# A transformer kernel on one core: attention loads issued at a set distance, three more x buffers, and a second residual loaded before the segment sums

## The chip, the cores and the metric

The kernel runs on one core of one Trainium2 chip. The time is the device time of one execution in microseconds (us); the kernel before has six timed runs. Lower is better. Beside them stands one execution that the hardware profiler recorded, and every duration below comes from it.

The names of the engines are those of the profile: PE is TensorE (PEld its weight loads), DVE is VectorE, ACT is ScalarE, POOL is GpSimd, and SP is SyncE, which here only issues DMA transfers. "SPq" in a line is an instruction of SP's queue.

## The reference, cut to what matters

x has 2048 tokens of 1024 numbers, in bf16. The result is `x + A(xn) + B(xn)` with `xn = layernorm(x)`:

```python
# A: attention in segments of 32 tokens; 32 heads of 128; mem are 8 rows that pass from segment to segment
h = concat([mem, xs]); q, k, v = h @ Wq, h @ Wk, h @ Wv
o = softmax(mask(q @ k.T * scale)) @ v        # mask: memory rows see all, tokens see memory and earlier tokens
o = o @ Wo; mem = o[:, :8]; outs.append(o[:, 8:])
# B: mixing along tokens, then an MLP of width 3584
h = gelu(layernorm(x) @ w1); hs = shift_tokens(h) @ w2      # four column groups, moved by -1, +1, -2, +2 tokens
x1 = x + hs
return x1 + gelu(layernorm(x1) @ w3) @ w4
```

The memory rows make the segments serial. The kernel replaces each segment's memory by one row worked out from the mean of the values, checks at the end that this was near enough, and has a serial path (lines 867 to 961) for the case that it was not; that path isn't taken here.

## The kernel before

The order of the work on PE, SP and POOL is the order in which the program is written (line 193); on DVE and ACT that holds in the first two phases only, and a scheduler places the instructions after them. Token tiles have 128 tokens, so there are 16 (n = 0 to 15).

**Phase one** (lines 222 to 363) normalizes x. `load_x` brings tile n into a ring of seven "xt" buffers by SP. Tiles 0 to 6 are loaded at the start, between w1 and w2; each later load is issued in `norm1`, seven tiles after the tile whose buffer it takes. The normalized tile is transposed on PE for n < 8 (line 290) and by a DMA transpose on SP for the others (line 274). PE multiplies with w1 (line 301).

**Phase two** (lines 366 to 391) multiplies with w2 (line 375), adds, normalizes again, and keeps x1 in a DRAM scratch tensor, R1.

**Phase three** (lines 393 to 552) is the MLP. It runs over four token blocks (tb) of four tiles. For each block PE computes 28 groups of eight matmuls with w3 (line 516), with ACT's gelu behind each, and then, for each tile and each half of 512 columns, one group of 28 matmuls with w4 (line 541). DVE adds each group to the residual tile R (line 542). All these groups use the four PSUM banks with the tag "mm", in turn: a group can start once the group four before it has been evicted. The residual of tile n comes by `load_r1` (lines 504 to 508): two loads on SP, R1 in fp32 (512 KB) and x in bf16 (256 KB), into rings of two buffers. POOL adds the two (line 537), and after DVE's evictions POOL stores the tile (line 552). Tile 0 is loaded before the blocks (line 510), and tile n + 1 when tile n is reached (line 533). In block 0, the groups f = 10 to 25 also call `seg_sums` (line 518), each of which puts a DMA transpose on SP (line 408) and a sum of it on DVE (line 410), also in a ring of two buffers.

**Phase four** (lines 561 to 605) computes the values V for all tokens (line 573) and stores them to DRAM.

**Attention** (lines 608 to 865) has five token blocks. The first four have four tiles of three segments (396 to 429 columns, the fourth with a small tile of one segment beside them), the last has five (495 columns). Each block has eight stages, one for each group of four heads. A stage is eight projections (`proj`, line 647, eight matmuls each): four with Wq, then four with Wk. The small work of the stage before is mixed in between them: `scores` of a tile (line 662) and `outputs` of a tile (line 686). After the scores, DVE and ACT make the softmax (lines 664 to 674), and SP issues the DMA transpose PT (line 677) that `outputs` needs. At the beginning of each block, PE works through the output projection of the block before (`Out.piece`, line 705).

The mixing is done by `tick`, which runs while the program is built: it keeps a clock of estimated PE time, `clock[0]`, adds the time of each projection to it, issues a load, and then writes out the scores and outputs that are due. The loads for the next stage are put into the list `loads` by `stage_loads`: two halves of Wq (512 KB each), two halves of Wk, and V with its memory rows (line 632 and following). `tick` takes one of them off the list each time it is called (`every = 1`), that is in the first five steps of a stage. What is left at the next stage's start is issued there at once (lines 765 and 766). The four "w" buffers hold Wq and Wk of this stage and the next, and there are three V buffers.

Of the kernel before, what the change touches and what calls it, by code (L numbers as in the profile page):

```python
# [15 lines left out]
BF16 = mybir.dt.bfloat16  # L16
# [7 lines left out]
P = 128  # L24
S = 2048
D = 1024
# [51 lines left out]
def kernel(  # L78
# [114 lines left out]
    with tc.manual_schedule(engines={mybir.EngineType.PE, mybir.EngineType.SP, mybir.EngineType.Pool}), ExitStack() as actx:  # L193
# [6 lines left out]
        with ExitStack() as bctx:  # L200
# [6 lines left out]
            def load_w3():  # L207

                c, k0 = divmod(w3_at[0], 4)
                w3_at[0] += 1  # L210
                cs = slice(c * (F // 2), (c + 1) * (F // 2))
                nc.sync.dma_start(w3_sb[:, 2 * k0:2 * k0 + 2, cs], w3_v[:, 2 * k0:2 * k0 + 2, cs])

            with ExitStack() as hctx:
# [7 lines left out]
                with ExitStack() as p0:  # L222
                    big = p0.enter_context(tc.tile_pool(name="p0big", bufs=1))
                    ring = p0.enter_context(tc.tile_pool(name="p0ring", bufs=3))
# [3 lines left out]
                    xts = {}  # L228

                    def load_x(n):  # L230
                        if n < NT:
                            xts[n] = ring.tile([P, D], BF16, tag="xt", bufs=7, name=f"xt{n}")
                            nc.sync.dma_start(xts[n][:], x_v[:, n, :])

                    load_x(0)
                    for c in range(4):
                        nc.sync.dma_start(w1_sb[:, :, c * 256:(c + 1) * 256], w1_v[:, :, c * 256:(c + 1) * 256])
                        if c == 1:
                            load_x(1)
                    for n in range(2, 7):  # L240
                        load_x(n)
                    for i in range(4):
                        nc.sync.dma_start(w2_sb[:, 2 * i:2 * i + 2, :], w2_v[:, 2 * i:2 * i + 2, :])

                    stats = {}

# [30 lines left out]
                    def norm1(n):  # L277
                        st, mv, ab, rr, nm2 = stats[n]
                        xn = xn_keep[n // 4][:, n % 4]
                        nc.vector.tensor_scalar(xn, xts[n][:], mv[:, 0:1], rr[:, 0:1], op0=ALU.subtract, op1=ALU.mult)  # L280
                        nc.gpsimd.dma_start(xn_v[:, n, :], xn)
                        load_x(n + 7)
                        if n in (12, 15):
                            load_w3()
                        return xn
# [80 lines left out]
                with ExitStack() as p2:  # L366
                    ring = p2.enter_context(tc.tile_pool(name="p2ring", bufs=4))
# [25 lines left out]
            with ExitStack() as p3:  # L393
# [3 lines left out]
                ring = p3.enter_context(tc.tile_pool(name="p3ring", bufs=2))  # L397
# [7 lines left out]
                def seg_sums(n):  # L405

                    xr = ring.tile([P, KT, P], BF16, tag="xr", name=f"xr{n}")
                    nc.sync.dma_start_transpose(xr[:], xn_v[:, n, :])
                    with nc.allow_low_precision(reason="sums are accumulated in fp32 and rounded once"):
                        nc.vector.tensor_reduce(xb[:, :, 4 * n:4 * n + 4], xr[:].rearrange("p k (s t) -> p k s t", t=SEG), axis=AX.X, op=ALU.add)  # L410
# [6 lines left out]
                def mem_start():  # L417
                    ps9 = psum3.tile([P, KT, M + 1], F32, tag="vr")
                    for k in range(KT):
                        nc.tensor.matmul(ps9[:, k, :], m0[:, k * P:(k + 1) * P], eye9[:], start=True, stop=True)  # L420
                    nc.vector.tensor_copy(MZ[:, :, 0:M], ps9[:, :, 0:M])
                    nc.vector.tensor_tensor(xb[:, :, 0:1], ps9[:, :, M:M + 1], xb[:, :, 0:1], op=ALU.add)
# [59 lines left out]
                def spec_load(depth=1):  # L482
                    while units and len(pending) < depth:
                        u, i = units.pop(0)
                        pending.append(u(i))
                        if u is unit_g and i == 7:
                            pending.append(unit_thr)

                def spec_step(depth=1):
                    if pending:  # L490
                        pending.pop(0)()
                    spec_load(depth)
# [3 lines left out]
                def load_wv():  # L496
                    hg = len(wvs)
                    if hg < 8:
                        wvs.append(wtile())
                        nc.gpsimd.dma_start(wvs[-1][:], Wv_v[:, :, hg * 512:(hg + 1) * 512])  # L500
# [3 lines left out]
                def load_r1(n):  # L504
                    if n < NT:
                        r1s[n] = (ring.tile([P, D], F32, tag="R1", name=f"R1_{n}"), ring.tile([P, D], BF16, tag="xt", name=f"xr{n}"))
                        nc.sync.dma_start(r1s[n][0][:], R1_v[:, n, :])
                        nc.sync.dma_start(r1s[n][1][:], x_v[:, n, :])

                load_r1(0)  # L510
                for tb in range(4):
                    depth = 1 if tb < 2 else 2
                    for f in range(FT):
                        ps = psum.tile([P, 512], F32, tag="mm", bufs=4)
                        for k in range(KT):
                            nc.tensor.matmul(ps[:].rearrange("p (n t) -> p n t", t=P), w3_sb[:, k, f * P:(f + 1) * P], xn3T[tb][:, :, k, :], start=(k == 0), stop=(k == KT - 1))  # L516
                        nc.scalar.activation(h3T[:, f, :], ps[:], ACTF.Gelu_apprx_tanh)  # L517
                        if tb == 0 and 10 <= f < 10 + NT:
                            seg_sums(f - 10)
                        if tb == 1 and f % 7 == 6 or tb > 1 and f % 5 == 4:  # L520
                            spec_step(depth)
                    if tb == 0:
                        spec_load()
                    if tb == 3:
                        w3ctx.close()
                        early = actx.enter_context(tc.tile_pool(name="aearly", bufs=1, side="right"))
                        vctx = ExitStack()
                        vph = vctx.enter_context(tc.tile_pool(name="vph", bufs=1, side="right"))
                        xT = vph.tile([P, NT, KT, P], BF16)
                    for j in range(4):  # L530
                        n = tb * 4 + j
                        R1, xt = r1s.pop(n)
                        load_r1(n + 1)
                        if tb == 3:
                            for m in range(4 * j, 4 * j + 4):
                                nc.sync.dma_start_transpose(xT[:, m], xn_v[:, m, :])
                        nc.gpsimd.tensor_tensor(R1[:], R1[:], xt[:], op=ALU.add)
                        for ch in range(2):
                            ps = psum.tile([P, 512], F32, tag="mm", bufs=4)
                            for f in range(FT):  # L540
                                nc.tensor.matmul(ps[:], h3T[:, f, j * P:(j + 1) * P], w4_sb[:, f, ch * 512:(ch + 1) * 512], start=(f == 0), stop=(f == FT - 1))  # L541
                            nc.vector.tensor_tensor(R1[:, ch * 512:(ch + 1) * 512], ps[:], R1[:, ch * 512:(ch + 1) * 512], op=ALU.add)  # L542
                        if n == NT - 1:
                            while pending or units:
                                spec_step(depth)
                        elif n == 3:
                            mem_start()
                        elif n > 3:
                            spec_step(depth)
                        if n == NT - 2:  # L550
                            load_wv()
                        nc.gpsimd.dma_start(R_v[:, n, :], R1[:])
# [161 lines left out]
        smalls = []  # L714
        clock = [0.0]
        flying = [0]
        turn = [0]
        every = 1
        loads = []

        def load_some(n):
            for _ in range(min(n, len(loads))):
                loads.pop(0)()
# [15 lines left out]
        def tick(us, blocked=None):  # L739

            clock[0] += us
            turn[0] += 1
            if turn[0] % every == 0:
                load_some(1)
            done = set()
            for item in list(smalls):
                due, kind, fn = item
                if due <= clock[0] and kind != blocked and kind[0] not in done and not (kind[0] == "S" and flying[0] >= 5):
                    smalls.remove(item)
                    flying[0] += 1 if kind[0] == "S" else -1  # L750
                    done.add(kind[0])
                    clock[0] += fn()
# [244 lines left out]
```

## Time and profile before

| | us |
|---|---|
| median of 6 runs | 1532.14 |
| lowest and highest run | 1529.63, 1536.52 |
| the profiled execution | 1531.0 |
| its span, from the first instruction to the last | 1529.1 |
| PE busy in that span | 1510.9 |
| mean granted clock of PE | 0.998 |
| phase one and two (0 to 125 us), PE busy | 121.5 |
| block 0 of the MLP (125 to 230 us), PE busy | 99.5 |
| values (544 to 764 us), PE busy | 218.9 |
| first block of attention (764 to 885 us), PE busy | 119.1 |

The page of a profile gives, for each engine, the time it was busy, and for groups of instructions the line of the kernel, the engine, the tiles written and read (`out<-in`), the count, the busy time and what ended the idle time before them. A wait line reads "who <- for whom: us in total, times, longest". A timeline lists instructions in order of time: start, length, engine, line, operation, tiles, count, and in brackets the idle time before it and what ended it. A window line gives for each engine the busy time in a stretch, then the granted clock of PE (1.00 is full speed), the busy share of the DMA engines and the GB/s that they moved. Matmuls are pipelined, so that consecutive ones overlap in the records.

### The profile page before, as it was taken

What the parts mean: (1) busy time and instruction counts of PE and PEld (TensorE: products, weight loads), DVE (VectorE), ACT (ScalarE), POOL (GpSimd) and SP (SyncE); (2) the same over time, 40 slices, a digit from 0 to 9 for tenths busy, and PEclk for the clock granted to TensorE, in tenths of its full rate; (3) what the DMA queues carried; (4) which work ended last, traced back from release to release, by engine and by line L of the source; (5) the groups of instructions that cost most, each with busy time, mean ns of one, the idle gap of its engine ahead of it and who ended that gap; (6) DMA issues with size and microseconds to landing.
All of it is one profiled execution on the core that took longest, in us unless ns stands there. A gap on an engine that the chain in (4) does not pass through costs nothing.

```text
span 1529.1 us, 24286 instructions
## 1 busy us (share of the span) xinstructions
PE 1510.9 (99%) x9781; PEld 808.7 (53%) x9853; DVE 546.0 (36%) x1137; ACT 506.6 (33%) x1147; POOL 179.3 (12%) x248
## 2 busy tenths in 40 slices
PE   9999989999999999999999999999999999999998
PEld 7744434455444444444455645664665555445555
DVE  8382230010020122211145624651564266416542
ACT  6433203103012011111156614650663266316630
POOL 5241020220211222100000010001000100010001
PEclk9999999999999999999999999999999999999999
DMA  8799762453345877632399955992897389628711
GB/s 267 171 254 328 198 170 90 145 186 111 128 161 143 210 256 255 223 124 83 124 238 236 246 136 163 240 250 70 236 245 196 104 220 220 194 67 210 180 42 57
DMA packets 306459, 274.20 MB, mean 179 GB/s; under 512 B 153787, under 2 KB 274128, under 8 KB 306088
## 3 DMA queue, kind: packets, MB, share of 16 engines
q1 hardware_dynamic: 284168, 189.92, 49.1%
q0 software_dynamic: 22032, 82.63, 15.8%
q8 instruction: 79, 1.29, 0.4%
q14 instruction: 36, 0.29, 0.1%
q10 hardware_dynamic: 144, 0.07, 0.0%
HBM read 190.98 MB, written 46.19 MB: 155 GB/s over the span
## 4 chain that ended last, share of the span: by engine, by line
PE 90%; DMA 5%; SPq 2%; DVE 2%; issue 1%; POOL 0%; ACT 0%; DVEq 0%; POOLq 0%; ACTq 0%
PE ps L647 29%; PE pso L705 14%; PE ps L573 14%; PE ps L541 10%; PE ps L516 9%; PE ps L375 4%; DMA xr<-xn_scratch 2%; PE ps L301 2%; PE psS L662 2%; PE psO L686 2%; SPq L415 1%; DMA PT<-Pn 1%; DMA xn2T<-xn 1%; DVE xb L410 1%; PE ps L467 1%
## 5 line engine op out<-in xcount | busy, mean ns | idle before, releaser
L647 PE MATMUL ps<-hTb,wt 128*128 128x396 bf16 (+3 forms) x2528 | 503.9, 343 | 0.0
L647 PEld LDWEIGHTS <-wt 128*128 128x128 bf16 x2528 | 231.0, 97 | 164.0
L573 PE MATMUL ps<-wt,xT 128*128 128x512 bf16 x1003 | 220.1, 379 | 1.1
L705 PE MATMUL pso<-wo_sb,oX 128*128 128x512 bf16 x938 | 209.5, 379 | 1.2 <-issue 0.2
L541 PE MATMUL ps<-w_sb,h3T 128*128 128x512 bf16 x873 | 196.5, 382 | 6.5 <-DVE R L542 5.3
L516 PE MATMUL ps<-xn3T,w_sb 128*128 128x512 bf16 x896 | 196.2, 379 | 0.0
L517 ACT ACTIVATE h3T<-ps 128x512 bf16<-128x512 f32 x112 | 66.8, 597 | 297.8 <-PE ps L516 296.9
L573 PEld LDWEIGHTS <-xT 128*128 128x128 bf16 x1024 | 100.2, 98 | 120.8
L653 ACT CAST KT<-ps 128x396 bf16<-128x396 f32 (+3 forms) x160 | 82.2, 514 | 224.3 <-PE ps L647 222.8
L705 PEld LDWEIGHTS <-oX 128*128 128x128 bf16 x960 | 92.6, 98 | 107.9
L541 PEld LDWEIGHTS <-h3T 128*128 128x128 bf16 x896 | 87.5, 98 | 110.3 <-issue 8.3
L516 PEld LDWEIGHTS <-w_sb 128*128 128x128 bf16 x896 | 86.6, 98 | 102.1
L668 DVE TENSOR_REDUCE sums<-sm 99x4 f32<-99x396 f32 (+2 forms) x176 | 97.6, 555 | 114.0 <-ACT sm L666 114.0
L664 DVE TENSOR_TENSOR sm<-psS,c_mask_reg_sb 99x396 f32<-99x396 f32 x160 | 91.2, 570 | 91.9 <-PE psS L662 91.4
L666 ACT ACTIVATE sm<-sm 99x396 f32<-99x396 f32 (+2 forms) x176 | 92.8, 527 | 72.1 <-DVE sm L664 71.5
L575 ACT CAST Vs<-ps 128x512 bf16<-128x512 f32 x64 | 37.5, 586 | 233.1 <-PE ps L573 174.9
L655 ACT ACTIVATE QT<-ps 128x396 bf16<-128x396 f32 (+3 forms) x160 | 84.2, 526 | 73.8 <-PE ps L647 54.0
L579 DVE CAST Vs<-ps 128x512 bf16<-128x512 f32 x64 | 44.3, 692 | 170.0 <-PE ps L573 158.0
L674 DVE TENSOR_TENSOR Pn<-sm,rs 99x396 bf16<-99x396 f32 (+2 forms) x176 | 98.9, 562 | 6.3 <-DMA PT<-Pn 0.3
L542 DVE TENSOR_TENSOR R<-ps,R 128x512 f32<-128x512 f32 x32 | 21.8, 689 | 185.9 <-PE ps L541 167.2
L712 POOL DMA_DIRECT2D out_dram<-ot x30 | 16.4, 546 | 585.5 <-DVE ot L711 579.7
L711 DVE TENSOR_TENSOR ot<-pso,Rt 128x512 bf16<-128x512 f32 (+1 forms) x33 | 22.3, 676 | 168.9 <-PE pso L705 163.7
(120 smaller groups left out, 1071.8 us busy)
## 6 DMA issues: line engine op xcount, KB each, us to landing
wt<-in_A_Wq_dram SPq DMA_DIRECT2D x76, 512.0 KB
wt<-in_A_Wk_dram SPq DMA_DIRECT2D x76, 512.0 KB
wt<-in_A_Wv_dram POOLq DMA_DIRECT2D x24, 1024.0 KB, 6.8
V_scratch<-Vs SPq DMA_DIRECT2D x32, 512.0 KB
V<-V_scratch SPq DMA_DIRECT2D x32, 384.0 KB
R_scratch<-x POOLq DMA_DIRECT2D x16, 512.0 KB, 4.3
R<-R_scratch SPq DMA_DIRECT2D x16, 512.0 KB
R_scratch<-R POOLq DMA_DIRECT2D x16, 512.0 KB, 3.1
```

The source lines that it names most:

```text
L516: nc.tensor.matmul(ps[:].rearrange("p (n t) -> p n t", t=P), w3_sb[:, k, f * P:(f + 1) * P], xn3T[tb][:, :, k, :], start=(k == 0), stop=(k ...
L517: nc.scalar.activation(h3T[:, f, :], ps[:], ACTF.Gelu_apprx_tanh)
L541: nc.tensor.matmul(ps[:], h3T[:, f, j * P:(j + 1) * P], w4_sb[:, f, ch * 512:(ch + 1) * 512], start=(f == 0), stop=(f == FT - 1))
L573: nc.tensor.matmul(ps[:], xT[:, m4 * 4 + j, k, :], wv[:, k, :], start=(k == 0), stop=(k == KT - 1))
L647: nc.tensor.matmul(ps[:, :nb] if flat else ps[:, :nb].rearrange("p (t c) -> p t c", t=nt), w[:, k, hh * P:(hh + 1) * P], B["rhs"](k), star ...
L653: nc.scalar.copy(o, i)
L655: nc.scalar.mul(o, i, scale)
L664: nc.vector.tensor_tensor(sm[:T, :, :T], S3, t["mask"][:].unsqueeze(1).to_broadcast((T, 4, T)), op=ALU.add)
L666: nc.scalar.activation(e[:T, :, :T], sm[:T, :, :T], ACTF.Exp, scale=LN2)
L668: nc.vector.tensor_reduce(ss, e[:T, :, :T], axis=AX.X, op=ALU.add)
L674: nc.vector.tensor_tensor(Pn[:T, :, :T], e[:T, :, :T], rs[:T, :].unsqueeze(2).to_broadcast((T, 4, T)), op=ALU.mult)
L705: nc.tensor.matmul(self.ps[:, :self.w], self.oX[self.gl // 3][:, h, self.gl % 3 * P:(self.gl % 3 + 1) * P], wo_sb[:, h, self.cc], start=(h ...
```

## The change

There are three edits, and none changes what PE computes or the order in which it does so.

1. The ring of x tiles in phase one has ten buffers instead of seven. Tiles 7 to 9 are loaded right after w2, and `norm1` loads tile n + 10 instead of n + 7.
2. The residual of tile 1 is loaded right after that of tile 0, before the first token block, and no longer when tile 0 is reached. From tile 1 on, tile n + 1 is loaded as before.
3. `tick` no longer issues a load each time it is called, but only when its clock is at least 2.2 us past the time at which `tick` last issued one (`PACE`). The rest is still issued at the next stage's start.

```diff
-                            xts[n] = ring.tile([P, D], BF16, tag="xt", bufs=7, name=f"xt{n}")
+                            xts[n] = ring.tile([P, D], BF16, tag="xt", bufs=10, name=f"xt{n}")
...
                         nc.sync.dma_start(w2_sb[:, 2 * i:2 * i + 2, :], w2_v[:, 2 * i:2 * i + 2, :])
+                    for n in range(7, 10):
+                        load_x(n)
...
-                        load_x(n + 7)
+                        load_x(n + 10)
...
                 load_r1(0)
+                load_r1(1)
...
                         R1, xt = r1s.pop(n)
-                        load_r1(n + 1)
+                        if n > 0:
+                            load_r1(n + 1)
...
-        turn = [0]
-        every = 1
+        PACE = 2.2
+        issued = [0.0]
...
             clock[0] += us
-            turn[0] += 1
-            if turn[0] % every == 0:
+            if clock[0] - issued[0] >= PACE:
+                issued[0] = clock[0]
                 load_some(1)
```

## The prediction

> **What bounds the kernel now.** I read the page's busy times first, then the waits of TensorE, then the timelines around the longest wait, and last one stage of attention.
>
> ```profile
> PE 1510.9 (99%) x9781; PEld 808.7 (53%) x9853; DVE 546.0 (36%) x1137; ACT 506.6 (33%) x1147; POOL 179.3 (12%) x248
> ```
>
> PE is busy for 1510.9 of 1529.1 us. The change keeps all PE instructions and their order, so it can win only from the 18.2 us of idle time and from a clock that idling lowers, while a new wait on PE costs its full length. The waits of PE:
>
> ```profile
> PE ps L541 <- DVE R L542: 5.3, 1, 5.3
> PE warm L318 <- DVE wz L312: 1.4, 1, 1.4
> PE psO L686 <- DMA PT<-Pn: 1.3, 2, 1.0
> ...
> PE psO L686 <- ACT QT L655: 0.6, 1, 0.6
> PE ps L301 <- DMA xn2T<-xn: 0.4, 2, 0.2
> ```
>
> One wait is worth speaking of. Its place, in the timelines of SP, POOL, DVE and PE (start, length, then the idle time before it and what ended it):
>
> ```profile
> 155.52 50.04 SPq L408 DMA_TRANSPOSE xr<-xn_scratch  x16
> 205.62 2.06 SPq L507 DMA_DIRECT2D R<-R_scratch  x1
> 207.72 0.43 SPq L508 DMA_DIRECT2D xr<-in_A_x_dram  x1
> ```
>
> ```profile
> 212.31 2.11 POOL L537 TENSOR_TENSOR R<-R,xr 128x1024 f32<-128x1024 f32 x1 [14.85 <-DMA xr<-in_A_x_dram]
> ```
>
> ```profile
> 214.45 1.29 DVE L542 TENSOR_TENSOR R<-ps,R 128x512 f32<-128x512 f32 x2 [4.14 <-POOL R L537]
> ```
>
> ```profile
> 173.50 36.42 PE L541 MATMUL ps<-w_sb,h3T 128*128 128x512 bf16 x164
> 215.19 14.27 PE L541 MATMUL ps<-w_sb,h3T 128*128 128x512 bf16 x55 [5.27 <-DVE R L542]
> ```
>
> The residual of token tile 1 (R1 and x, lines 507 and 508) stands on SP behind sixteen transposes, which take 50 us. So it is issued at 205.62, POOL adds at 212.31, DVE evicts at 214.45, and PE, whose four "mm" banks are full, stands from 209.92 to 215.19. A table of windows shows what follows (the 0.50 is the granted clock):
>
> ```profile
> 212.50:219.30 6.80, 4.11 (x10) 1.43 (x10) 1.52 (x3) 0.00 (x0) 4.63 (x3) 0.50 0.26 104
> ```
>
> In attention PE idles for about 2 us in all. There SP is the queue to look at. One stage in the middle of block 2, which PE starts at 1119.23, as SP issues it:
>
> ```profile
> 1121.78 0.58 SPq L734 DMA_DIRECT2D wt<-in_A_Wq_dram  x1
> 1123.62 1.19 SPq L677 DMA_TRANSPOSE PT<-Pn  x1
> 1124.86 0.57 SPq L734 DMA_DIRECT2D wt<-in_A_Wq_dram  x1
> 1125.53 0.47 SPq L734 DMA_DIRECT2D wt<-in_A_Wk_dram  x1
> 1126.73 1.19 SPq L677 DMA_TRANSPOSE PT<-Pn  x1
> 1127.97 0.59 SPq L734 DMA_DIRECT2D wt<-in_A_Wk_dram  x1
> ```
>
> [...] an idle time of 5.27 us brought 6.8 us at 0.50, while the waits of 1.0 us and less brought none. [...] the trace has 3.8 to 3.9 us for a half weight load on a quiet queue (below), and I use this. [...]
>
> **The change, part by part.**
>
> *Second residual ahead of the segment sums.* R1_1 and x_1 move on SP from behind the sixteen transposes to before them. The wait of 5.27 us goes, and with it the half clock: between 215.19 and 219.32 PE worked 4.13 us at 0.50, which loses 2.06 us. Together 7.3 us. What is late next: the moved loads are 512 + 256 KB in front of the transposes, at the 298 GB/s moved in the window 125 to 174 us that is 2.6 us; at worst SP's issue of them is held as long as that of tile 0 (3.75 + 1.47 us). So transposes and sums run 2.6 to 5.2 us later. In the built order on DVE the evictions of tile 1 stand after 13 and 16 sums. The 13th ended near 200.1 and the 16th at 210.3; 2.6 us later that is 202.7 and 212.9. PE wants these banks at 209.5 and 215.5 (groups of 28 matmuls, 6.0 us), so both are in time. Tile 3's residual needs the buffer of tile 1, free about 3 us after its store: store 213.6, landed 216.7, load 4.4, add 2.1 on POOL, evicted 224.4, against some 225.3 when PE wants that bank for the next token block. In time by 0.9 us at the low delay, late by 1 to 2 us at the high one. I take 0.5, ends 0 and 2.
>
> *Ten x buffers.* Loads of tiles 7 to 9 are issued at once, and the six others before the eight DMA transposes of line 274, which stood among them and behind their waits on DVE (16.6 us on SP). PE sees of this only 0.4 us (0.2 us twice, before line 301). What these loads move past on SP is those transposes alone: w1 and w2 stay in front of them, and the w3 loads behind. I take 0.3 won, ends -0.2 (x tiles crowding the first transposes) and 0.4.
>
> *Paced loads, what they take away.* PE's 1.9 us of waits for PT and QT in block 0 fall where SP issued loads in bursts (a transpose issued there took up to 2.5 us, against 1.19). Spread, I take 1.5 of it gone, ends 0 and 1.9.
>
> *Paced loads, what they add.* A projection with its small matmuls takes 1.54 us, so 2.2 us is passed at every second one: each stage of eight issues loads after its 2nd, 4th, 6th and 8th projection, and the V load with the next stage. In the built order each weight half stands behind the transpose of one tile's scores. A transpose issues 3.03 to 3.07 us after its scores' first matmul (the DVE and ACT chain) and takes 1.19, so the load behind it goes out 4.3 us after the scores. For the stage above (scores at 1120.58, 1123.66, 1126.73, 1129.80): first Wq half 1124.86 (was 1121.78), second 1127.97 (was 1124.86), first Wk half 1131.0 (was 1125.53), second 1134.1 (was 1127.97). PE needs them at 1131.36, 1132.03, 1137.5 and 1138.2 (weights are loaded one matmul ahead). That leaves 6.5, **4.06**, 6.5 and **4.09** us to land. The slack of the two first halves is ample; the two second halves meet the 3.8 to 3.9 us of a lone load with 0.2 us to spare. Doing this for every stage gives 35 such tight loads, all in blocks 0 to 2; in blocks 3 and 4, with longer projections and five tiles, 4.5 us and more are left.
>
> The page gives no landing for SP's loads; I took the last of each DMA's 16 semaphore updates in the trace. Of 40 half loads that stand behind a transpose, with the load before them landed at most 1.3 us after their issue, thirty took 3.7 to 4.09 us, and ten exceed 4.09, by 0.1 to 1.83 and by 6.5 in all: 6.5 / 40 = 0.16 us for each load. Ten of 152 issues of line 734 took 1.3 to 1.9 us instead of 0.57: less the slack 10 / 152 x 0.7 = 0.05. So 0.21 us of stall for a tight load, 35 x 0.21 = 7.4 us. A stall gives the next tight load as much more time, and about a quarter of the loads stall, so I take three quarters: 5.5 us. Ends: 0 (latencies at 3.85) and 21 (below). V, now issued a few us later, is read a stage later still: nothing.
>
> **Sum**: -7.3 + 0.5 - 0.3 - 1.5 + 5.5 = -3.1 us. The profiled execution took 1531.0 us (span 1529.1), the median of the runs is 1532.1, 1.1 more; on the median the sum gives **1529.0**, beside 1527.9 for the profiled execution.
>
> **The rivals.**
> *No stalls in attention.* The bursts are gone, DMA latencies stay near 3.85. For it: thirty of 40; block 0's DMA share of 0.98 falls. Against: the slack is 0.2 us, and 35 loads have to meet it. 1532.1 - 7.3 + 0.5 - 0.3 - 1.5 = 1523.5, say 1523.
> *Slower: the second halves of Wq and Wk land late, so PE waits in nearly every stage of blocks 0 to 2.* In the present bursts the other 73 such loads took 4.9 us at the median, and 5.3 and more in the upper third. If spread loads still need this, each is 0.8 to 1.2 us late, and as one stall shelters the next, the 35 make 17.5 stalls: 14 to 21 us, middle 17.5. 1532.1 - 8.6 + 17.5 = 1541. For it: the time allowed was cut by 3 us for Wq and 6 us for Wk. Against: the queue is quieter. It decides from 8.6 / 17.5 = 0.5 us a stall; from there the kernel is slower.
> *The residual doesn't do it.* The delayed transposes hold up tile 1's second or tile 3's eviction by as much as is now lost, the clock falls again: -0.3 - 1.5 + 5.5 = 3.7 us over, 1536. Against: the margins of 1 to 6 us above.
>
> **How the numbers follow.** What a measurement can tell from no change is about 0.2%, 3.1 us, so the bounds are 1529.1 and 1535.2. Forecast 45% (its own range 1525 to 1534), no stalls 20%, late halves 25%, residual fails 10%. Faster: half of the forecast and the second, 0.45 with rounding up; within 0.2%: the rest of the forecast and half of the last, 0.27; slower 0.28. The range goes from 1521, under the best case, to 1543, inside the slower one; that leaves out some 5% below and 13% above.
>
> **What would show it.** Waits of PE: no "ps L541 <- DVE R" of some us and no window at 0.50 near 215 us, else the first step is wrong. Waits of "ps L647" for a DMA of wt, 0.2 to 1.8 us each, some 10 to 20 of them, none over 2.5 us and no lowered clock. If they are absent, the second case holds; if there are over 15 us of them, the third. SP's transposes in attention should all take near 1.2 us, 3.07 apart.

## The result, and the profile after

The kernel became slower. Its median is 1537.51 us in 17 runs (1533.59 to 1543.21), and the kernel before has 1531.94 us in 38 runs (1528.75 to 1536.52). The ratio is 1.0039, with a 95% interval of 1.003 to 1.0047. The forecast was 1529.0 us; the measured time is near the rival "second halves of Wq and Wk land late" (1541). The profiled execution of after took 1540.06 us, with a span of 1538.2 us, so it is 9.1 us longer than the profiled one of before.

TensorE's busy time grew by 2.6 us and its idle time by 6.5 us (the line of before is in the prediction). The instructions are the same 9781:

```profile
PE 1513.5 (98%) x9781; PEld 807.3 (52%) x9853; DVE 545.4 (35%) x1137; ACT 506.0 (33%) x1147; POOL 179.1 (12%) x248
```

The waits of TensorE, after (who <- for whom: us in total, times, longest). The lines of the kernel have moved by four: line 651 is the projection that was 647, line 545 the matmul with w4 that was 541.

```profile
PE ps L651 <- DMA wt<-in_A_Wq_dram: 7.4, 10, 1.5
PE ps L651 <- DMA wt<-in_A_Wk_dram: 5.7, 7, 2.4
PE warm L320 <- DVE wz L314: 1.4, 1, 1.4
PE ps L292 <- DVE xn L273: 0.7, 2, 0.4
```

Two things are to be seen. The 5.3 us for R at the w4 matmuls are gone, and so are the 1.9 us for PT and QT. In their place are 13.1 us for the weights of attention, which before had no line at all.

**The boundary of block 0.** The timelines of SP, POOL, DVE and TensorE, for the place where before stood still from 209.92 to 215.19:

```profile
151.07 3.33 SPq L509 DMA_DIRECT2D R<-R_scratch  x1
154.44 1.42 SPq L510 DMA_DIRECT2D xr<-in_A_x_dram  x1
155.91 1.20 SPq L509 DMA_DIRECT2D R<-R_scratch  x1
157.16 0.64 SPq L510 DMA_DIRECT2D xr<-in_A_x_dram  x1
```

```profile
197.58 2.14 POOL L541 TENSOR_TENSOR R<-R,xr 128x1024 f32<-128x1024 f32 x1
```

```profile
204.20 0.68 DVE L546 TENSOR_TENSOR R<-ps,R 128x512 f32<-128x512 f32 x1
211.90 0.68 DVE L546 TENSOR_TENSOR R<-ps,R 128x512 f32<-128x512 f32 x1
```

```profile
173.99 48.51 PE L545 MATMUL ps<-w_sb,h3T 128*128 128x512 bf16 x219
222.43 0.35 PE L422 MATMUL ps<-c_eye_sb,m 8*128 8x9 bf16 x8
```

The residual of tile 1 is issued at 155.91 and no longer at 205.62. POOL adds it at 197.58, DVE evicts at 204.20 and 211.90, and TensorE runs through all w4 matmuls of the block in one piece. The stretch from the first w3 matmul to the first matmul behind the block (line 422) took 104.24 us before and takes 96.79 us now, 7.45 us less.

**Attention.** TensorE begins it 6.97 us earlier than before (757.39, before 764.36), and needs 16.1 us more from there to its end. I measured every projection from its first matmul to its fifth, where the second half of a weight is first needed. Before, none of the 320 shows a stall there; after, 24 do, with 16.7 us together. The wait lines show only 17 and 13.1 us: records of consecutive matmuls overlap (0.33 us long, 0.17 us apart), so about 0.17 us of each stall lies under the record of the matmul ahead of it, and a shorter one isn't listed. That is also part of why "busy" grew. By block of attention (lengths in us, between the first projections of two blocks; for block 4 to its last matmul):

| block | before | after | stalls after |
|---|---|---|---|
| 0 | 99.71 | 102.63 | 5.25 |
| 1 | 139.96 | 141.75 | 1.84 |
| 2 | 139.79 | 148.10 | 6.58 |
| 3 | 150.20 | 153.30 | 3.06 |
| 4 | 164.23 | 164.23 | 0 |

The largest stall, in the timelines of SP and TensorE (after, block 2):

```profile
1102.74 1.19 SPq L681 DMA_TRANSPOSE PT<-Pn  x1
1103.97 0.59 SPq L738 DMA_DIRECT2D wt<-in_A_Wq_dram  x1
1106.47 1.19 SPq L681 DMA_TRANSPOSE PT<-Pn  x1
1107.71 0.57 SPq L738 DMA_DIRECT2D wt<-in_A_Wk_dram  x1
1109.54 1.19 SPq L681 DMA_TRANSPOSE PT<-Pn  x1
1110.78 1.04 SPq L738 DMA_DIRECT2D wt<-in_A_Wk_dram  x1
1111.91 0.47 SPq L636 DMA_DIRECT2D V<-V_scratch  x1
```

```profile
1114.34 0.84 PE L651 MATMUL ps<-hTb,wt 128*128 128x396 bf16 x4
1117.60 1.50 PE L651 MATMUL ps<-hTb,wt 128*128 128x396 bf16 x4 [2.42 <-DMA wt<-in_A_Wk_dram]
1118.89 0.54 PE L666 MATMUL psS<-KT,QT 128*99 128x99 bf16 x4
```

Each half stands directly behind a transpose, as the prediction's example had it. The second half of Wk goes out at 1110.78. In a projection without a stall the fifth matmul starts 0.68 us after the first, here at 1115.02, and its weights are wanted one matmul, 0.17 us, earlier: 4.1 us were allowed. The half took 6.77 us, its semaphore updates end at 1117.55, and TensorE starts the second four matmuls at 1117.60. They take 1.50 us, where the four before took 0.84: the clock was halved. The window there confirms it (0.51 is the granted clock, 0.80 the busy share of the DMA engines):

```profile
1117.30:1120.80 3.50, 3.20 (x13) 1.72 (x14) 0.66 (x2) 1.03 (x2) 0.00 (x0) 0.51 0.80 225
```

### The profile page after: what moved, and what is told of

The parts are those of the page before. It is cut to its first block, busy times and chain, and to the rows that moved or that the text cites. A ratio compares the mean times of both kernels' runs of the same rounds, so it can differ in the third digit from the quotient of the medians.

```text
span 1538.2 us, 24233 instructions
## 1 busy us (share of the span) xinstructions
PE 1513.5 (98%) x9781; PEld 807.3 (52%) x9853; DVE 545.4 (35%) x1137; ACT 506.0 (33%) x1147; POOL 179.1 (12%) x248
## 4 chain that ended last, share of the span: by engine, by line
PE 91%; DMA 6%; SPq 1%; issue 0%; ACT 0%; DVE 0%; POOL 0%; ACTq 0%
PE ps L651 25%; PE pso L709 14%; PE ps L577 14%; PE ps L519 13%; PE ps L545 12%; PE ps L377 4%; PE ps L303 3%; DMA wt<-in_A_Wq_dram 3%; DMA wt<-in_A_Wk_dram 3%; PE psS L666 2%; PE psO L690 2%; SPq L681 1%; PE ps L841 1%; PE ps L469 1%; PE ps L434 0%; PE gps L448 0%
## 5 line engine op out<-in xcount | busy, mean ns | idle before, releaser
L651 PE MATMUL ps<-hTb,wt 128*128 128x396 bf16 (+3 forms) x2528 | 509.2, 344 | 13.2 <-DMA wt<-in_A_Wq_dram 7.4
L651 PEld LDWEIGHTS <-wt 128*128 128x128 bf16 x2528 | 229.4, 98 | 183.8 <-DMA wt<-in_A_Wq_dram 13.1
```

The source lines that it names most:

```text
L651: nc.tensor.matmul(ps[:, :nb] if flat else ps[:, :nb].rearrange("p (t c) -> p t c", t=nt), w[:, k, hh * P:(hh + 1) * P], B["rhs"](k), star ...
```

## The experiments

**My theory** after the result: the residual and the ten buffers did what they should; the loss is entirely from the pacing, because it issues second halves of the weights so late that their landing, longer than I had taken it, comes after TensorE needs them. **Rivals**: the loss is from an interplay of the edits; or the spread loads became slower for themselves (more crowding with V and PT), so that an earlier issue would not help.

Ratios are against the kernel before, run beside the experiment, with their 95% intervals in brackets. Edits are against the changed kernel unless said otherwise.

### e1: residual and ten buffers, no pacing

```diff
-            if clock[0] - issued[0] >= PACE:
-                issued[0] = clock[0]
-                load_some(1)
+            load_some(1)
```

> The changed kernel with a load at each step again, as before (the first two edits alone). If the paced loads cost all of the loss: 1522 to 1525 us, that is 7 us under the kernel before, with no wait of PE for wt. If something of the first two edits costs as well (phase one took 0.5 us more in the profile of the change): above 1527 us.

Measured: 1523.26 us (1522.54 to 1524.12, 6 runs), before 1530.11; ratio 0.9947 (0.9932 to 0.9963). The waits of TensorE, e1:

```profile
PE psO L690 <- DMA PT<-Pn: 2.6, 2, 1.5
```

No line of e1 names a weight of attention, and no projection shows a stall at its fifth matmul. The 2.6 us for PT are those of the bursts, all in block 0 (100.28 us long). So edits 1 and 2 win 7 to 8 us (6.9 by the medians, 8.1 by the ratio), and edit 3 turns that into a loss: it costs 14.3 us between the medians of e1 and of after.

### e2: pacing alone

The kernel before, with edit 3 of the diff only.

> The kernel before with the paced loads alone. If pacing costs 13 to 16 us by itself: 1545 to 1548 us, and the waits of PE at the second halves as in the change. If it costs only together with the other edits: under 1540 us.

Measured: 1542.68 us (1539.09 to 1554.24, 7 runs); ratio 1.0075 (1.0058 to 1.0091). This is 12.6 us over the median before (1530.11), and a little under the 1545 to 1548 that were expected. The profiled execution is the longest of the seven. Its waits of TensorE (lines as in the kernel before):

```profile
PE ps L541 <- DVE R L542: 11.9, 1, 11.9
PE ps L647 <- DMA wt<-in_A_Wq_dram: 6.9, 11, 1.7
PE ps L647 <- DMA wt<-in_A_Wk_dram: 4.7, 7, 1.6
```

The weight waits are there without the other two edits: 21 stalls, 15.15 us in all, against 24 and 16.7 in after. So no interplay is needed for them, and the medians add up: 12.6 us lost here and 6.9 won in e1 make 5.7 lost, where the change lost 5.6. The 11.9 us in the first line is the wait of the kernel before, 5.3 us there and 4.3 us in e5, in one profiled execution of each. The traces with the early residual (after, e1, e3, e6, e7) have no such wait.

### e3: the same pacing, begun one step earlier

```diff
                 if loads:
                     load_some(len(loads))
+                issued[0] = clock[0] - PACE
```

The distance between loads stays at 2.2 us; only the first load of a stage goes out at its first step, so each half stands behind the transpose ahead of the one that it stood behind in after.

> The changed kernel with the pacing clock set back at each stage's start, so that the loads go with steps 1, 3, 5 and 7, not 2, 4, 6 and 8: on SP one transpose earlier, 3.1 us, at the same distance. If the loss is that second halves go out too late by some us: it vanishes, 1522 to 1526 us, although a load takes as long from issue to landing as in the change. If spreading the loads among the transposes costs PE by itself: 1535 us or more.

Measured: 1521.56 us (1521.06 to 1523.04, 6 runs); ratio 0.9939 (0.9924 to 0.9954). The waits of TensorE, e3:

```profile
PE warm L320 <- DVE wz L314: 1.4, 1, 1.4
PE ps L292 <- DVE xn L273: 0.8, 2, 0.5
PE ps L303 <- ACT xn2T L296: 0.3, 1, 0.3
```

SP in block 2, e3:

```profile
1100.89 1.19 SPq L681 DMA_TRANSPOSE PT<-Pn  x1
1102.13 0.58 SPq L738 DMA_DIRECT2D wt<-in_A_Wq_dram  x1
1104.01 1.19 SPq L681 DMA_TRANSPOSE PT<-Pn  x1
1105.24 0.58 SPq L738 DMA_DIRECT2D wt<-in_A_Wk_dram  x1
1107.08 1.19 SPq L681 DMA_TRANSPOSE PT<-Pn  x1
1108.31 0.58 SPq L738 DMA_DIRECT2D wt<-in_A_Wk_dram  x1
```

TensorE starts the stage that needs these halves at 1108.80, and its fifth projection at 1114.94. The second half of Wq, issued at 1102.13, has until 1109.3 to land, 7.2 us, and the second of Wk, issued at 1108.31, until 1115.4, 7.1 us. In after the pair of 1103.97 and 1110.78 had 4.7 and 4.1 us. This is the test between lateness and slow transfers, and it is clear: the second halves took *longer* to land in e3 (median in blocks 0 to 2: Wq 5.37, Wk 4.84 us; after 4.59 and 4.29), and yet only two projections stall, by 0.44 us together. The rival "slower transfers" falls; the lateness stands. Not a single PT wait is left either: block 0 takes 97.56 us, 2.15 less than before.

### e4: V loaded once in a block

```diff
-            Vs = [qkv.tile([P, len(B["tiles"]), 512], BF16, tag="V", bufs=3, name=f"V{B['b']}") for B in Bs]
+            if hg == 0:
+                kept_V[:] = [qkv.tile([P, len(B["tiles"]), 512], BF16, tag="V", bufs=3, name=f"V{B['b']}") for B in Bs]
+            Vs = list(kept_V)
...
-            for B, V in zip(Bs, Vs):
+            for B, V in zip(Bs, Vs) if hg == 0 else ():
```

This kernel uses the values of the first head group for all of a block's heads, so that seven in eight V loads fall away.

> The changed kernel, V loaded in the first stage of each block only and reused (so values of other heads are left out). If the V load just ahead of each stage is what makes the half loads take 4.6 and 4.3 us and not 3.85: they fall to some 3.9, and PE's stalls at second halves from 16.7 us to 6 or less. If the half loads are slow by themselves: over 12 us of stalls stay.

Measured: 7305.29 us in a single execution, which says nothing of the loads, because the values left out send the kernel into its serial path after attention. Up to there the trace can be read. TensorE's waits in the first 1530 us, e4:

```profile
PE ps L651 <- DMA wt<-in_A_Wq_dram: 6.4, 6, 2.0
PE ps L651 <- DMA wt<-in_A_Wk_dram: 3.4, 5, 1.2
```

17 stalls with 12.27 us are left of 24 with 16.7. That is about a quarter less, and the sum stays just over the 12 us that the expectation set as the mark of a small part. It compares one execution with one: after and e2, whose loads in attention are paced alike, already differ by 1.5 us, so the quarter for V is an estimate. Medians of landing fall to 4.15 (Wq) and 3.98 us (Wk), still close to the time allowed.

### e5, e6: ten buffers alone, residual alone

Each is the kernel before with one edit of the diff.

> The kernel before with the ten x buffers alone. Expected: no difference that can be told, within 1 us. The rival, that the earlier x loads delay the first groups of phase one (0.5 us later in the profile of the change), would give 1 us or more over the kernel before, with the first matmul with w2 starting at 70.4 us or later.

Measured: 1530.71 us (1525.49 to 1542.35, 22 runs), before 1530.07 (30 runs); ratio 1.0005 (0.9992 to 1.0018). The rival's sign is absent too: the first matmul with w2 starts at 69.10 us, before at 69.90. The waits, e5: the boundary is untouched.

```profile
PE ps L543 <- DVE R L544: 4.3, 1, 4.3
```

> The kernel before with the second residual loaded early, alone. Expected: 7 us under the kernel before (the wait of 5.3 us and the half clock of 2 us gone), no wait of PE at the MLP's matmuls with w4. If the two edits without pacing needed each other: less than 4 us.

Measured: 1524.35 us (1523.17 to 1532.67, 9 runs); ratio 0.9966 (0.9945 to 0.9987). TensorE at the boundary, e6:

```profile
174.55 48.51 PE L543 MATMUL ps<-w_sb,h3T 128*128 128x512 bf16 x219
223.00 0.35 PE L420 MATMUL ps<-c_eye_sb,m 8*128 8x9 bf16 x8
```

Again one piece. The residual is the whole gain of e1 within the intervals, and the ten buffers are worth nothing that 22 runs can show.

### e7: residual and early steps, seven buffers

Edit 1 is taken back from e3.

> Seven x buffers as before, the early second residual, and the pacing clock set back at each stage's start (loads with steps 1, 3, 5, 7). If the x buffers are worth nothing: as with them, 1521 to 1523 us beside 1530 for the kernel before; if they matter: 1 us or more from that.

Measured: 1521.85 us (1521.33 to 1522.49, 6 runs); ratio 0.9943 (0.9925 to 0.9961). It equals e3 within the intervals, so the better version than both kernels is the early residual with a pace that starts at the first step, 8 to 9 us under before (8.2 by the medians, 0.0057 x 1530 = 8.7 by the ratio); the x buffers may stay at seven.

### e9: all loads one transpose later than after

```diff
                 if loads:
                     load_some(len(loads))
+                issued[0] = clock[0] + 3.0
```

> The changed kernel with each load one transpose later on SP (steps 4, 6, 8, and the rest with the next stage), 3.1 us. If the time left to the second half of Wq decides, it falls from 4.1 to 1.0 us, while a load still takes some 4.5 us: a stall of 3 to 4 us in each of some 23 stages of blocks 0 to 2 and 1 to 3 us in those of block 3, so 1590 to 1630 us. If pacing costs by its mixing of loads and transposes and not by lateness: about as the change, 1535 to 1545 us.

Measured: 1649.95 us in a single execution, span 1648.1, mean granted clock 0.972. This is more than the range that I had given. The waits, e9:

```profile
PE ps L651 <- DMA wt<-in_A_Wq_dram: 78.0, 46, 3.6
PE ps L651 <- DMA wt<-in_A_Wk_dram: 0.3, 1, 0.3
```

Waiting grew from 13.1 to 78.3 us, nearly all of it for Wq: the halves of Wk go out together behind a stage's last transpose or at the next stage's start, and are needed only from that stage's fifth projection on. Attention takes 127 us longer than before, and the listed waits explain 78 of these, or some 86 with the 0.17 us by which each of the 47 is listed too short. The rest is the clock, for which the expectation had nothing: (1 - 0.972) x 1648 = 46 us is the most that it can have cost. The trace has 92.2 us at half clock, and TensorE worked in 84 of them, so an estimated 42 us were lost. TensorE, e9:

```profile
1040.15 0.85 PE L651 MATMUL ps<-hTb,wt 128*128 128x396 bf16 x4 [2.34 <-DMA wt<-in_A_Wq_dram]
...
1052.37 0.85 PE L651 MATMUL ps<-hTb,wt 128*128 128x396 bf16 x4 [0.43 <-DMA wt<-in_A_Wq_dram]
1055.43 1.50 PE L651 MATMUL ps<-hTb,wt 128*128 128x396 bf16 x4 [2.21 <-DMA wt<-in_A_Wq_dram]
...
1057.07 2.38 PE L651 MATMUL ps<-hTb,wt 128*128 128x396 bf16 x8
```

Four matmuls take 0.85 us after the first two stalls and 1.50 after the third; eight take 2.38 where they took 1.52. So the same loads one transpose later than in after cost some 112 us (1650 less 1537.5), and one transpose earlier they win some 16 (1521.6 less 1537.5): after stands at the bend of that curve.

## Why the prediction was wrong, point by point

- **Second residual** (-7.3, and +0.5 of new lateness): right. The stretch became 7.45 us shorter, and no eviction came late. Alone it gave 0.34% (e6), with the ten buffers 0.53% (e1), that is 5 and 8 us, around the 6.8 forecast (the difference between the two isn't shown, their intervals overlap). DVE evicted at 204.20 and 211.90, where 202.7 and 212.9 were worked out.
- **Ten x buffers** (-0.3): right, nothing that can be measured (e5).
- **PT and QT waits in block 0** (-1.5): right in kind, a little small. Block 0 lasts 99.71 us before and 97.31 to 97.56 in e3 and e7, where hardly a stall hides it: 2.15 to 2.4 us.
- **Stalls of paced loads** (+5.5): this is the step that failed. The mechanism was right (second halves behind a transpose, with 4.1 us to land), and the term failed in its size: 5.5 us were put for 35 tight loads, and it measured 16.7 us of stalls, and the clock after the largest stall lost 1.7 more (half of 3.4 us). All together, on the profiled execution: -7.0 up to attention, then +16.7 + 1.7 - 2.3 = +16.1; 1531.0 + 9.1 = 1540.1, which is the time that it took. This execution is 2.5 us over the median of its kernel; by the medians of after and e1, pacing cost 14.3 us net, where +5.5 and -1.5 make 4.0.

Where did the 5.5 come from? The prediction took the landing of a half load from 40 loads that were quiet: the load before them had landed 1.3 us after their issue at the latest. Thirty of these took 3.7 to 4.09 us. That picked the sample by the property that was to be shown. Of 40 tight loads in blocks 0 to 2 of after (35 had been counted) only 18 were quiet by this measure, with a median of 4.04 us and seven over the 4.09 allowed. The 22 others had a median of 4.81, and 21 of them exceeded it. Held against the time that each had, the 18 were late by 0.17 us in the mean, as the prediction says of quiet loads (0.16), and the 22 others by 0.61 us. So what failed is the assumption that all tight loads would be quiet. The other 73 loads of before, with 4.9 us at the median, stood in the prediction as the rival's case and were left out of this term. Over all 113 loads the mean excess over 4.09 us is 0.70 us, and the prediction's own sum gives 35 x 0.70 x 3/4 = 18.4 us with it, near the 16.7 measured. What is more, block 3 was called safe with 4.5 us and more to land, and its stalls cost 3.06 us: 1.65 of them in its first stage, whose second halves go out in block 2 with 4.1 and 5.4 us to land, and 1.4 in two stages where 4.5 and 6.5 us were not enough. The sentence that no stall would lower the clock was the author's estimate: the waits of before that it had were one of 5.27 us, with half clock, and those of 1.0 us and less, without. It failed as well, once in after (2.42 us).

The rival of the late halves had it, also by the sign that was set for it (over 15 us of stalls): 14 to 21 us in 17.5 stalls, against 16.7 us in 24. A single stall was shorter than it said (0.8 to 1.2 us forecast, 0.7 measured) and there were more of them, so that its sum came so near is in part luck.

**What stays open**: why more than half of the paced loads still meet another. V is about a quarter of the stalls by the estimate of e4. In after, the remainder of a stage is issued at its start beside a PT transpose. Behind the largest stall's loads, SP spent 1.99 us on the transpose at 1112.88, where those of the timeline above took 1.19, and the two halves of Wq behind it, issued at 1114.92 and 1116.94, took 5.62 us each to land, against 4.6 at the median of all halves of after. What lengthened them is not shown: the shares of PT, of V and of the first halves were not separated.

## What to carry to other kernels

On SP's queue, which here issued in the order of the program, a load was as late as what stood in front of it: the residual of tile 1 went out at 205.62 behind the sixteen transposes (50.04 us, before) and at 155.91 ahead of them (after). So for each load, count the time from where it can issue behind that to where it is needed, and hold this against the upper part of the landing times under the traffic that will be there (up to 7.2 us in after), not against the quiet ones (in before, 3.7 to 4.09 us for thirty of 40). If the margin is a few tenths of a us, the even distance isn't worth having; start the series one step sooner and keep the distance (here 1521.6 instead of 1537.5 us). An edit that removes a burst and one that delays a load are two things, even when one line of code does both.

## What the hardware showed that was not expected

The granted clock fell to half after a stall shorter than the one of before. In after, TensorE stopped at 1115.18 and went on at 1117.60; the clock was at half from 1117.35 to 1120.76, that is from 2.17 us after the stop on, and for 3.41 us. In before, TensorE stood from 209.92 to 215.19, and the clock was at half from 212.49 to 219.32, from 2.57 us after the stop on, and for 6.83 us. The other stalls of after, up to 1.46 us, left it at full.

The length of a stall alone did not tell which one came with half clock. By the four matmuls directly behind each stall of a projection:

| trace | stall, us | matmuls behind it, from | four of them take, us | clock |
|---|---|---|---|---|
| after | 1.46 (the second longest of after) | 795.03 | 0.86 | full |
| after | 2.42 | 1117.60 | 1.50 | half |
| e9 | 2.34 | 1040.15 | 0.85 | full |
| e9 | 0.43 | 1052.37 | 0.85 | full |
| e9 | 2.21 | 1055.43 | 1.50 | half |

In e9 2.21 us came with half clock and the longer 2.34 us did not. The one of 2.21 had one of 0.43 us 3 us ahead of it; whether that decided it is not shown, and no safe length of a stall can be read from these traces.

Nor was the landing time a constant of the size: halves of 512 KB took 3.7 to 7.2 us on the same queue in after, and up to 8.7 in e3, where they did no harm.
